# Gate arithmetic of a fused GateLoop + PReLU-MLP kernel: small operations from GpSimd to VectorE, the state decay from VectorE to ScalarE, first gates in halves, an early activation, a new order

## The chip, the core and the metric

The kernel runs on one core of a Trainium2 chip. The core has five engines with a queue each, and each queue runs strictly in its order: TensorE (PE; its weight loads are shown as PEld), VectorE (DVE), ScalarE (ACT), GpSimd (POOL) and SyncE (SP, which here issues the DMAs). The metric is the device time of one execution in microseconds, the median of several runs. One execution was also profiled, instruction by instruction; its trace begins at 0 and its last instruction ends at the span.

## What is computed

```python
# q, k, v, a_re, a_im: 4 batches x 8 heads x 768 tokens x 48
mag = np.sqrt(a_re * a_re + a_im * a_im)
scale = np.minimum(mag, 0.999) / (mag + 1e-06)
a_re_n, a_im_n = (a_re * scale, a_im * scale)
...
for t in range(S):
    new_re = ar * S_re - ai * S_im
    new_im = ar * S_im + ai * S_re
    kv = np.einsum('bhd,bhe->bhde', k[:, :, t], v[:, :, t])
    S_re, S_im = (new_re + kv, new_im)
    y[:, :, t] = np.einsum('bhd,bhde->bhe', q[:, :, t], S_re)
...
h = x @ w_in                                   # x: y as 3072 x 384; w_in: 384 x 2048
g = np.maximum(h, 0.0) + alpha * np.minimum(h, 0.0)
return (g @ w_out).astype(np.float32)          # w_out: 2048 x 384
```

A complex gate per head, token and feature makes a state decay and turn; each token adds its key-value product and reads the state with its query. The result goes through an MLP with a PReLU.

## The kernel before, in words

The program is a set of Python generators, each one a strand of work that stops at every `yield`. A long string `ORDER` (L30) names with one letter after another which strand goes on by one step (`Plan.run`, L99). So the order of each engine's queue is written out by hand, letter by letter; a wait between engines is a semaphore that the framework puts where a tile is read after it is written.

**Gates** (`gates`, L228) run nine times, called g0 to g8 here: 128, 256 and 384 tokens of batch 0, then two times 384 tokens of each other batch. One set has all 8 heads x 48 features on 128 partitions, in three groups, so 384, 768 or 1152 elements a partition. A set does, in this order: magnitudes and square roots (ScalarE L259 to L287, VectorE L265 to L307); a tree of decay products by halves (L324), sent to memory as `decs`; a running product of the turned unit numbers, first within 8 tokens (L344 multiplies, L346 adds, seven times), then over 8 such blocks (again seven times, 72 and 36 elements), then step by step along the blocks (12 and 6 elements, six times for 384 tokens), with ScalarE copies between (L372, L374); then the products for the offsets (L402, L405), a correction of length (L413, L415, L417), and at last the full phases (VectorE L432, L435), sent to memory as `phs`. What is at most `SMALL` = 80 elements a partition, and what is written with `tiny`, goes to GpSimd, except in g0, where it goes to VectorE:

```python
tiny, tiny_engine = (DVE, nc.vector) if g < 1 else (POOL, nc.gpsimd)
```

**Weights** (`to_f32`, L500) come as float64 words and are turned to float32 in 16 pieces, `w_in` and `w_out` in turn: ScalarE L513, L515, L517; GpSimd L521; VectorE L523, L525. The GpSimd step stands in the same queue as the small gate operations, and VectorE L523 waits for it.

**Units** (`unit`, L649) are the 24 blocks of 128 tokens, u0 to u23, six to a batch. Each loads phases (`PP`) and decays (`T`) from memory, turns queries and keys (VectorE L667, L669), then six times decays them by half-blocks (VectorE L722), with ScalarE copies (L745, L761) for TensorE's small products (L684) and masks (VectorE L707, ScalarE L698). The state is kept in `St`, twice a unit: multiplied by its decay on VectorE (L834, 96x384), then the key-value products from PSUM are added (VectorE L837). ScalarE copies the output (L863), and it goes through memory into the MLP's `xT`.

**The MLP** (`features`, L889) makes for each 128 or 256 tokens and each of 16 blocks of features three products on TensorE (L897), a Relu on ScalarE (L904) and the PReLU on VectorE (L906, 160 of them); the block's output product (L916) follows on TensorE. The last three groups of 256 tokens use sums of blocks in place of some products (L1016, L1028 to L1060, L1079, L1091). "The n-th PReLU" below is the n-th L906 in VectorE's queue.

Of the kernel before, what the change touches and what calls it, by code (L numbers as in the profile page):

```python
# [9 lines left out]
F32 = mybir.dt.float32  # L10
# [3 lines left out]
AF = mybir.ActivationFunctionType  # L14
# [16 lines left out]
    "AABMBAMAAJAJAAAAAAABMMJJAAAAABABAAKAAAAAABABAAAAKABAKABAMALNABLLABBBMLABBLABLBNKABOAKNNABAMAOANLBBAA"  # L31
    "AAOOAAAABMAANKBLAAABKAANAABAABAOBAAAANABABABABALNNAAKAOAAAAAOMAOKAAAOOAABABLNKBNBNCBNCBJBNNBJBJBLBBO"
    "BOBBBBNBCNBBCBPBCBBOCBPPLKMKKCBMCKBBPJBPCKKPPCJBBPOPOOBBBOMBLPPBBKCCBBJNOKBBJPKPKPBBPBNBBCBBBCCBBBCC"
    "PCPBCBOBNNCOMBBBPKBLOOPCMBBPCPBCNBPPPPPBCOOCONPDCNDCJCNCCCCCPPKOCLPCOPCCNNOCMCJDNJCJCDNDKCCPCDCCNCCK"
    "QDCMPDCCCPDCCPCNCPCPPOQPDCNLPLCCDCJNCDJPPPQLPLOQQLCPQCDNCCQMCCDLDCCJPOQCPPCQPCCJCDDLDLOLNOOnDLCCJQJD"
    "DLOQQLRQJoKOOOoJOoQLDKRCCCCCoCJCooooQQLCoQDCNoooQRoCCNCoLQRCCRoKRNNQJQQMQQoooooQDQQoQRDooQoQooCoQQDC"
    "DooQCoRRDQDNQOoRLLDNLRRoLRCoNLLooooRoLoNMooooQoLRRNNCLLRLKCRLRQCRRRoRRRLRLQLoQQQoDQoQQORQQDoQROoJoRD"
    "RoooORDJDJoDoRDoORoRDoOODRSoLJoDoESoJDJESLLRSSDnSOLDooDoSDoDJDDDDDoRLDSSDJDoSDKKooooSSRDoLENDLRRRDNK"
    "DoRRLRooooORDoRSoREooKSooELoSSJELoLooooooEooSJoLoEoTSLSDLoDSSDKSSDSLoooSKDTDoooooSSSJooooEoDTDJoETDD"
    "oooSoTSToDTDEEoEDooooSoDSTTDEDSESSoDLDooETLoooLSTLEDDDDoJDDDLSDoooTToooLSDJooTooLooLSSSTLSTooJEooLoo"  # L40
    "LSoooSToLSoDLoDoooSEooSToLTLooETTEDooJoTUTTJToTDooooTJoDoTnKEoooooTDoToooooDToTUDTTTDLLoooooULoLoooU"
    "oDLoJoLDooUoUDUooooJoUUJooooLoTEULoLooooUKoEUJoTULooEFoUoLoTLoEFUUELETTELUoooooToUVTUoooUUTTUTTUoTUo"
    "EEooooEoVoJoUJEUVooooUEJoUEJoEEooUoUooEUoEFUUEUoUFEoLELoFEoLoEJFEJEoELoooooEVLEoVJELUVLEoooooVFLVEUU"
    "EVLEUoLUooEoVVEoEUVoUEUUoUoooVEWVFEVoVoEEnEoJEVVEJEooooEoEFKVELoLooVEEVFKEoLoVVVVoLEoJVWEoooEKWEEVVK"
    "FLJooooVoWEEEFooooWWoWJEVoJoJooVWWoEVWoFoVWEVFFoEVEVoEFVVFWVLWLEWELoooLoVoLFoLLWWoLVVoEVWLoVVFoVVVoV"
    "oEFoLWoLWooLWWWWWoFLoELWLWWoJoEJoWXEoooooooEEJJEJoooWoWoooFEoooWoWEXWoWJWoXLoKoWXLWoLFoooWXLXWWGXWLo"
    "WFoGoXXWLXWWoLooooLXoFXJXWoXLoLFXXFFoooooFXFoLoGFLWFLooooXFXLoLXXXXoXXoFXGFoooXonXFoJFoJXoFXJoooFGJX"
    "FJGJXoFGooFYoGFooooooFXYFoFGFoooJYFXoXXLYFLXFFLXFXLFFLFFLFFoooYYooYYYooooXFXLFYoKXFoXFKGYFFoLXXooYYo"
    "XFYFXoLoYYoFFGFFoJGJYFLooooooLYFZoFFYLGLYFYJYYYLYoooooFYZJooGKoooZJYFoFYKoGFFFFoZLFZJoZYJZKYZZoooooG"
    "GoYoZYYGZYYFZLFZooLZLoGLooLoZZLGFoZGLFLGoooLYLoYGooooZZYLYYYoLooZZYZLoYZLZoYaYYoLZoFYZZFGoFZFoooaZoZ"  # L50
    "FoJoJZoFJZZoZFZoLLGoFFoLooFnoLaLLooooooaJFaoJaaLJGFaaGGooooooGLaLZGaLZoooooooaGoaZHZZZLaZJHoooLoaaoo"
    "ZaZoZZGZoooaoGaooGoaaaaaaoLoLaGGoooaoaKbooaoGHGooooJGaoHoGbbaKHaJaGJaoaGLHLLooooHoGLobLoGHLooobJoGoG"
    "LoaGGbGGGJbaobGHKaoGbGaJoLbboGKHGoLaaoLobGJKHHbGLoHLoooobboGLbaGoaaaobLbLooooHboJoGGcKobGbGGJbbbbGbJ"
    "bbJoooobGHGooboboGbGGobGHHGcGbobGHbGGboLcLonoHcoJoLcobcLGGGGGooGbJGocHJGoLoccoLGbLHLcoLbcLooooobHbLd"
    "cLcbobcbbbLoooobccoLoLGcHoJoHGJooccocccGccGoccJoHoGJcoJcGHGHooococoocoGHGJHcccooHdoodooGdoGooocodLdc"
    "GdoooLoHLoddLooooLdooodIooocLoHLocoIcdLoHdcLdcLcJoooddKoHcLcdoooccoooIcHLddHLoHIoLdoLIJeoJdddoooooJd"
    "HodKdIdodJoooJHdJodHoIoHdHIHddeodIdooJIoLLooHLeoHLHoHoooeHIHoIoooodKeHeodLHHdKHeHKHLdddHLooooHoeeHLo"
    "HeHLodLoooeofnHoHdLHedHHIeLHoeHddodeeHHooooHoHIeHoJoIHLJooooeIHIeLHoJoJeeeeeHoKeeIJJoooeoeoLoIooooII"
    "ofooHefJoHeHHoooffIHfeHfIHooffoIofoooeoefgoeHefLfIoLfoLoILeoILoooHffLoHgoLIoLoeHLooofLoIoIoeLfoeLfHe"
    "fffLHeffLfeIHeHeIeefooooHooefoIfLoooIoIoJoHJfofKoooJHoooIHHoJJooooHoofoIHffffIgLLoooLgoIgHgfoLgoLoLg"  # L60
    "gLoooIoJfoooogLoLoogfJfffgLgIfoLffgofffoLoIggLKogoooooLgIJgoIJggggIJIgIoJpggIooogogogogoIhIooggggIhh"
    "JJngIoLgoJIohLIogLIhoILLoogghIhLgIhgIogLhIgogohhoLiIgIoILhIoooooohJIiIhoLhLhIJooooLIhhoIILoIhIJoLooo"
    "IhLIhIJIhoIhooohoJhihhJhhoIIIJhooopIiohohiihiIoioiooooIioIohihIohIohjiLIiIoLiLoLohonioLoiLooohLohoLi"
    "oLoLhhhioIhiLhohihLioiIiIiohiohLoILoiiLiooopJooJoJioioooIooiIIiiiiijoLILoLjLLiooooooooojooJoILooLjiL"
    "jojJoIoooLjjoJojoLLiijiLjoijoLiojiLioLjiojioJojoooojjJojjjjJojjoJjpjoJjJooojojokojokjjojkjoLjLkojLkk"
    "JokoJoLkkLjoLkLjLkooojjojojojjjlkojkLooLokokkJkJoooooooooJooLkoLkoonkkkkkLokkJolookkolLLooookllklolo"
    "llooooooloklkokokkkokLLkoLkooLoLlolokLlkLoLlloLokJlkoJoLokoooJpLooLookooololoollkoLomkoLllLlooololpo"
    "loJoJplmooololoolollllmoooomlolomomoomoommoomoooomololomomolmlolmlolmoooonloooLmLoLoLmomooommmmLomoo"
    "LooLoooomoLoLoolooLoomLooooooqLooLooLoooooomomooooooooomoooooooooooooooooooomoooooooooooooooomomomoo"
    "moomooomomopomomoqlmqmqmmmqqmqqqooooooqoqooooqoqqoqooqqoqooqooqqqqooqqoooqoqooooqoqqoqooqqooooooooqo"  # L70
    "ooooooqoqooooooooooqooqoqoqqoqoooqonqqoqooqoqqooqoqoqqqqoqqooooooooooqoqqoooooooooqoooooooooqoqqoooo"
    "ooqoooooooqoqoqooqoqqqqoqqoooooooooooooooqqqoqoqoqqqoqoqooooooooqqoqqooooooooqqoqqoqooqooooooooqoqqq"
    "ooooooqoqqoqooqoqooqqoqooooqoooooooqoqqoooooooooooqooooqqoooqoqqoqooqoqooqqoqoqqqoqoooqqqqooqoooooqo"
    "qqoqooqoooqqooooooqoooooooooooqoqooooooooooooqqqqoqqoooooooooooooooqqqooqoqqoqqoqoqoqoooooooqooqqooo"
    "qqooooqoqqooooooooqooooqqooooooqqoqqooooooooqoooooooqoooqoqqqoqoooooooooqqqoqooooqoooqqoqqoqooqoqooq"
    "oqqqqqqqqqqqqqqqqqqqqqqqqqqq")
# [28 lines left out]
def kernel(  # L105
# [120 lines left out]
    nc.vector.memset(bias_half, -0.5)  # L226

    def gates(g, b, c0, c1):  # L228
# [8 lines left out]
        tiny, tiny_engine = (DVE, nc.vector) if g < 1 else (POOL, nc.gpsimd)  # L237
# [7 lines left out]
        flat = work.tile([P, 6 * NK * GT], F32, tag="gate", name="gate", bufs=2)[:, 0:6 * N]  # L245
# [3 lines left out]
        for z, src in ((x, a_re), (y, a_im)):  # L249
            z = z.rearrange("p (t s) -> p t s", t=NK)  # L250
            rows = src[b].rearrange("n i d s -> (n i d) s").rearrange("(t p) s -> p t s", p=P)
            t = yield DMA(N / 2, ("gates", g - 2))
            nc.sync.dma_start(z[:, :, 0:n - last], rows[:, :, c0 * P + 1:c1 * P + 1 - last])

        t = yield ACT(N, t)
        if last:
            ends_ = G[:, 0:6:5].rearrange("p r (t s) -> p r t s", t=NK)[:, :, :, n - 1]
            nc.scalar.activation(ends_, ident[:, 0:2 * NK].rearrange("p (r t) -> p r t", r=2), AF.Copy, scale=0.0)
        nc.scalar.activation(x, x, AF.Identity, scale=1.5, bias=bias_tiny)  # L259
        yield ACT(N)  # L260
        nc.scalar.activation(c, x, AF.Square, scale=GATE_SCALE)
        t = yield ACT(N, t)
        nc.scalar.activation(d, y, AF.Square, scale=1.5 * GATE_SCALE)
        t = yield DVE(N, t)
        TT(out=c, in0=c, in1=d, op=ALU.add)  # L265

        t = yield ACT(N, t)
        nc.scalar.activation(d, c, AF.Abs_reciprocal_sqrt)
        t = yield ACT(N, t)
        nc.scalar.activation(e, d, AF.Square)  # L270

        te = yield ACT(N, t)
        nc.scalar.activation(f, e, AF.Abs_reciprocal_sqrt)
        t = yield DVE(N, te)
        TT(out=e, in0=e, in1=c, op=ALU.mult)
        t = yield DVE(N, t)
        STT(out=d, in0=e, scalar=3.0, in1=d, op0=ALU.subtract, op1=ALU.mult)
        tf = yield ACT(N)
        nc.scalar.activation(f, f, AF.Square, scale=ONE / (1.5 * GATE_SCALE * MAG_EPS), bias=bias_one)
        tf = yield ACT(N)  # L280
        nc.scalar.activation(f, f, AF.Abs_reciprocal_sqrt)
        tf = yield ACT(N)
        nc.scalar.activation(f, f, AF.Identity, scale=ONE / 2.0, bias=bias_half)
        ts = yield DVE(N, t)
        TT(out=c, in0=c, in1=d, op=ALU.mult)
        ts = yield ACT(N, ts)
        nc.scalar.activation(c, c, AF.Copy, scale=1.0 / (1.5 * GATE_SCALE))  # L287

        L = 8
        nb = N // L  # L290
# [889 lines left out]
```

## Time and profile before

| | us |
|---|---|
| median of 3 runs (lowest, highest) | 836.75 (834.86, 837.43) |
| the profiled execution's own time | 839.4 |
| its span | 837.7 |
| busy PE / PEld / DVE / ACT / POOL | 689.3 / 544.4 / 695.3 / 441.3 / 321.6 |

A row of the profile's groups reads: line, engine, operation, tile written <- tiles read, shape written <- shape read, how many; then busy us and mean ns of one; then the engine's idle time ahead of them and what ended it. The part in 40 slices gives the busy share of each slice (20.9 us) in tenths. The chain of waits follows the work that ended last back from the end; a window of it is a list of start, duration, engine, tile and line. The view of waits gives for each engine and line what it waited for: us in total, times, the longest.

### The profile page before, as it was taken

What the parts mean: (1) busy time and instruction counts of PE and PEld (TensorE: products, weight loads), DVE (VectorE), ACT (ScalarE), POOL (GpSimd) and SP (SyncE); (2) the same over time, 40 slices, a digit from 0 to 9 for tenths busy, and PEclk for the clock granted to TensorE, in tenths of its full rate; (3) what the DMA queues carried; (4) which work ended last, traced back from release to release, by engine and by line L of the source; (5) the groups of instructions that cost most, each with busy time, mean ns of one, the idle gap of its engine ahead of it and who ended that gap; (6) DMA issues with size and microseconds to landing.
All of it is one profiled execution on the core that took longest, in us unless ns stands there. A gap on an engine that the chain in (4) does not pass through costs nothing.

```text
span 837.7 us, 27535 instructions
## 1 busy us (share of the span) xinstructions
PE 689.3 (82%) x11680; PEld 544.4 (65%) x11680; DVE 695.3 (83%) x1074; ACT 441.3 (53%) x946; POOL 321.6 (38%) x448
## 2 busy tenths in 40 slices
PE   0000225888999999999999999999999999999997
PEld 0000224666777777677766777777776777899997
DVE  5977978999898999899998999998897676546574
ACT  8767777557556746673666477344433334212121
POOL 5378397448203800860193037216100000324332
PEclk9999999899999999999999999999999999999999
DMA  6793876695686679548875875687466442100000
GB/s 186 222 266 120 279 210 154 216 224 143 170 247 143 178 191 259 137 124 236 216 203 123 249 174 152 174 214 187 98 189 146 125 119 58 34 27 20 1 20 20
DMA packets 186595, 130.97 MB, mean 156 GB/s; under 512 B 74728, under 2 KB 176872, under 8 KB 186088
## 3 DMA queue, kind: packets, MB, share of 16 engines
q1 hardware_dynamic: 186472, 129.20, 57.4%
q8 instruction: 92, 1.51, 0.8%
q14 instruction: 31, 0.25, 0.1%
HBM read 100.82 MB, written 35.71 MB: 163 GB/s over the span
## 4 chain that ended last, share of the span: by engine, by line
PE 55%; DVE 22%; POOL 12%; ACT 5%; issue 4%; DMA 2%; DVEq 0%; ACTq 0%; POOLq 0%; SPq 0%
PE ps_o L916 16%; PE ps_h L897 15%; PE ps_m L1091 6%; DVE KQ L722 4%; POOL gate L344 4%; PE ps_lv L684 4%; PE ps_y L1016 3%; PE ps_h L1016 3%; DVE gate L344 3%; POOL run L346 3%; POOL gate L346 3%; PE ps_y L825 2%; DVE gate L346 2%; PE ps_y L849 2%; PE ps_kv L805 2%
## 5 line engine op out<-in xcount | busy, mean ns | idle before, releaser
L916 PE MATMUL ps_o<-w_out_sb,g_sb 128*128 128x384 f32 x576 | 226.7, 510 | 7.4 <-DVE g_sb L906 7.3
L897 PE MATMUL ps_h<-xT,w_in_sb 128*128 128x256 f32 (+1 forms) x960 | 228.0, 369 | 0.0
L897 PEld LDWEIGHTS ps_h<-xT,w_in_sb 128*128 128x128 f32 x960 | 172.7, 195 | 49.4 <-issue 3.1
L722 DVE TENSOR_TENSOR KQ<-KQ,T 96x1024 f32<-96x1024 f32 x120 | 148.7, 1239 | 23.4 <-PE ps_lv L684 17.1
L916 PEld LDWEIGHTS ps_o<-w_out_sb,g_sb 128*128 128x128 f32 x576 | 103.9, 194 | 48.3 <-DVE g_sb L906 8.6
L904 ACT ACTIVATE g_sb<-ps_h 128x256 f32<-128x256 f32 (+1 forms) x160 | 57.5, 361 | 104.7 <-PE ps_h L897 104.1
L684 PE MATMUL ps_lv<-WQ 96*32 96x32 f32 x2304 | 35.0, 204 | 78.0 <-DVE WQ L667 53.4
L1079 POOL TENSOR_TENSOR sums<-g_sb 128x128 f32<-128x128 f32 x48 | 21.8, 475 | 192.0 <-DMA ysc<-T 117.5
L684 PEld LDWEIGHTS ps_lv<-WQ 96*32 96x32 f32 x2304 | 26.7, 116 | 99.2 <-DVE WQ L667 53.4
L906 DVE SCALAR_TENSOR_TENSOR g_sb<-g_sb,al,ps_h 128x256 f32<-128x256 f32 (+1 forms) x160 | 71.1, 445 | 22.2 <-ACT g_sb L904 20.5
L344 POOL TENSOR_TENSOR gate<-gate 128x72 f32<-128x72 f32 (+1 forms) x56 | 35.0, 626 | 140.7 <-ACT gate L374 102.6
L745 ACT COPY WQ<-KQ 96x1024 f32<-96x1024 f32 x48 | 50.0, 1041 | 27.0 <-DVE KQ L722 26.8
L324 POOL TENSOR_TENSOR gate<-gate 128x72 f32<-128x72 f32 (+5 forms) x24 | 13.1, 547 | 109.1 <-DVE gate L324 102.6
L761 ACT COPY W<-KQ 96x512 f32<-96x512 f32 x48 | 30.8, 641 | 42.7 <-DVE KQ L722 36.6
L684 PE MATMUL ps_lv<-KQ,W 96*32 96x32 f32 x1536 | 24.8, 206 | 33.4 <-ACT W L761 33.2
L521 POOL TENSOR_SCALAR top<-top 128x768 f32<-128x768 f32 x16 | 41.8, 2617 | 23.7 <-ACT top L513 23.7
L344 DVE TENSOR_TENSOR gate<-gate 128x576 f32<-128x576 f32 (+3 forms) x70 | 46.1, 659 | 1.1
L825 PE MATMUL ps_y<-A,VL 64*48 64x64 f32 x2304 | 41.8, 221 | 5.4 <-issue 5.4
L344 POOL TENSOR_TENSOR gate<-run,runs 128x12 f32<-128x12 f32 x46 | 39.3, 854 | 15.0 <-ACT runs L374 11.7
L432 DVE TENSOR_TENSOR gate<-gate 128x1152 f32<-128x1152 f32 (+2 forms) x36 | 44.7, 1263 | 0.1
L825 PEld LDWEIGHTS ps_y<-A,VL 64*48 64x48 f32 x2304 | 38.8, 123 | 8.9 <-issue 8.8
L684 PEld LDWEIGHTS ps_lv<-KQ,W 96*32 96x32 f32 x1536 | 20.2, 116 | 35.2 <-ACT W L761 34.7
(157 smaller groups left out, 1435.6 us busy)
## 6 DMA issues: line engine op xcount, KB each, us to landing
T<-decs SPq DMA_DIRECT2D x48, 384.0 KB
PP<-phs SPq DMA_DIRECT2D x24, 387.0 KB
KQ<-in_q_dram SPq DMA_DIRECT2D x48, 192.0 KB
decs<-gate SPq DMA_DIRECT2D x7, 1152.0 KB
phs<-gate SPq DMA_DIRECT2D x14, 576.0 KB
KQ<-in_k_dram SPq DMA_DIRECT2D x40, 192.0 KB
vsc<-in_v_dram SPq DMA_DIRECT2D x48, 144.0 KB
VL<-vsc SPq DMA_DIRECT2D x48, 144.0 KB
```

The source lines that it names most:

```text
L344: on(4 * k).tensor_tensor(out=m, in0=w[:, 1::-1].unsqueeze(2).to_broadcast([P, 2, 2, k]), in1=pairs_of(u), op=ALU.mult)
L346: on(2 * k).tensor_tensor(out=dst, in0=m[:, 0], in1=m[:, 1], op=ALU.add)
L684: nc.tensor.matmul(t[64 * i + j:64 * i + j + HC // 2, p], lhsT=keys(n, g), rhs=queries(n, g), start=True, stop=True)
L722: nc.vector.tensor_tensor(out=x, in0=x if x0 is None else x0, in1=m, op=ALU.mult)
L745: nc.scalar.copy(z.rearrange("p i n t -> p i (n t)").rearrange("p i (m h) -> p m i h", h=h), bass.AP(tensor=KQ.tensor, offset=KQ.offset + ...
L825: nc.tensor.matmul(o, lhsT=Vp[h][64 * i:64 * i + 64, s, e_ * D:(e_ + 1) * D], rhs=a, start=False, stop=False)
L897: nc.tensor.matmul(p, lhsT=w_in_sb[:, f // 2, kk, f % 2 * P:(f % 2 + 1) * P], rhs=x_of[m][:, kk], start=(kk == 0), stop=(kk == NK - 1))
L904: nc.scalar.activation(gt, p, AF.Relu, scale=-1.0)
L906: nc.vector.scalar_tensor_tensor(out=gt, in0=gt, scalar=al_1[:, f:f + 1], in1=p, op0=ALU.mult, op1=ALU.add)
L916: nc.tensor.matmul(sums[0], lhsT=gt[:, c * P:(c + 1) * P], rhs=w_out_sb[:, f], start=(f == 0), stop=(f == NF - 1))
L1016: nc.tensor.matmul(o, lhsT=lhs, rhs=rhs, start=(at in (0, 5)), stop=(at in (4, 8)))
L1091: nc.tensor.matmul(banks[k][:, half], lhsT=lhs, rhs=rhs, start=(j == 0 and half == 0), stop=(j == NF // 2 - 1 and at in (2, 3, 5, 6)))
```

## The change

1. `tiny` is VectorE for every set. With it all operations of L324 to L417 that ran on GpSimd go to VectorE; GpSimd keeps the small memset L311, the weights' L521 and the late sums L1079.
2. g0 (384 elements) is worked in two halves of 192 for the magnitude and the root; its `x` no longer waits for `a_im`; the copies of the unit numbers come in six halves, ahead of what the decays need.
3. Sets of 128 and 256 tokens make the unit numbers ahead of the decays; g1's three rows then lie in a part of the gate tile of their own.
4. An activation of one column (`Abs_reciprocal_sqrt`) is the first instruction of ScalarE.
5. From unit 4 on the state times its decay is made by eight ScalarE activations of 96x48, one per head, with the decay as scale, in place of L834.
6. `ORDER` is another string, so that every queue has a new order.

```diff
+    nc.scalar.activation(consts.tile([P, 1], F32, tag="first", name="first"), bias_two, AF.Abs_reciprocal_sqrt)
...
-        tiny, tiny_engine = (DVE, nc.vector) if g < 1 else (POOL, nc.gpsimd)
+        tiny, tiny_engine = DVE, nc.vector
...
+            for h in range(2):
+                yield from enter(h)
+            for h in range(2):
+                yield from root(h)
...
-        U5 = G[:, 0:3].rearrange("p r (m n i) -> p r m n i", m=L // 2, i=2)
+        U = G[:, 0:3] if C > 2 else flat_[:, 6 * N:9 * N].rearrange("p (r n) -> p r n", r=3)
+        U5 = U.rearrange("p r (m n i) -> p r m n i", m=L // 2, i=2)
...
+            def enter(h):
+                x, c, f, d, e, y = parts[h]
+                yield ACT(N // 2, tx)
+                nc.scalar.activation(x, x, AF.Identity, scale=1.5, bias=bias_tiny)
...
-            k_ = yield DVE(H * D, known, takes=(R["St"],))
-            St = work.tile([D2, H, D], F32, tag="St", name="St", bufs=3)
-            nc.vector.tensor_tensor(out=St, in0=before, in1=T[0:D2, :, TL - 4 + s:TL - 3 + s].to_broadcast([D2, H, D]),
-                                    op=ALU.mult)
+            if u < 4:
...
+            else:
+                k_ = yield ACT(5 * H * D, known, takes=(R["St"],))
+                St = work.tile([D2, H, D], F32, tag="St", name="St", bufs=3)
+                for n in range(H):
+                    nc.scalar.activation(St[:, n], before[:, n], AF.Copy, scale=T[0:D2, n, TL - 4 + s:TL - 3 + s])
```

## The prediction

> **What bounds the kernel now.** First the part in 40 slices, to see which engine is full when.
>
> ```profile
> PE   0000225888999999999999999999999999999997
> ...
> DVE  5977978999898999899998999998897676546574
> ...
> POOL 5378397448203800860193037216100000324332
> ```
>
> TensorE is nearly idle for six slices (to about 126 us), then full to the end. VectorE is full between about 140 and 600 us too, and has holes before. So two questions count: when TensorE's full stretch begins, and whether VectorE can feed it. From the first PReLU (138.2 us) to the end are 699.5 us; TensorE's rows behind that point, each at its group's mean and scaled to the 689.3 us busy, are 679. From the 37th PReLU (243.4 us) on 593 us of work stand against 594.3: **from there nothing is lost any more**. Both orders have, within 3 us, the same TensorE work behind each PReLU. So the time is that of the 37th PReLU plus 594.3, if VectorE keeps up after it.
>
> Next, the chain of waits in the window 88 to 140 us, to see why TensorE begins so late (start, us, engine, tile, line).
>
> ```profile
> 118.71 0.24 POOL gate L344
> ...
> 119.02 5.47 POOL run L346
> ...
> 124.56 2.09 POOL gate L344
> ...
> 129.53 2.10 POOL top L521
> ...
> 131.66 0.03 DVE top L523
> ...
> 135.37 1.42 DVE KQ L722
> ...
> 138.15 0.34 DVE g_sb L906
> ```
>
> From 104 to 131.6 us all of it is GpSimd: g2's small operations, one by one, and behind them in the same queue the weights' L521, for which VectorE's L523 waits, with unit 1 and the PReLUs behind it. The waits of VectorE between 53 and 140 us give the price:
>
> ```profile
> DVE top L523 <- POOL top L521: 10.2, 3, 3.9
> DVE gate L307 <- ACT gate L287: 4.6, 1, 4.6
> ```
>
> Then the groups by shape, for what an operation costs on each engine:
>
> ```profile
> L346 POOL TENSOR_TENSOR run<-gate 128x6 f32<-128x6 f32 x46 | 39.5, 858 | 3.6
> ...
> L344 POOL TENSOR_TENSOR gate<-gate 128x72 f32<-128x72 f32 x49 | 28.6, 584 | 137.2 <-ACT gate L374 102.6 <-ACT A L698 31.3
> ```
> ```profile
> L834 DVE TENSOR_TENSOR St<-St,T 96x384 f32<-96x384 f32 x44 | 25.4, 578 | 0.2
> ...
> L344 DVE TENSOR_TENSOR gate<-gate 128x24 f32<-128x24 f32 x7 | 1.3, 181 | 0.2
> ...
> L346 DVE TENSOR_TENSOR run<-gate 128x6 f32<-128x6 f32 x2 | 0.3, 164 | 0.0
> ```
> ```profile
> L698 ACT ACTIVATE A<-ps_lv,columns 128x64 f32<-128x64 f32 x96 | 23.3, 315 | 9.5 <-PE ps_lv L684 9.3
> ```
>
> The same 6-element addition takes 858 ns on GpSimd in the mean (0.20 us at its shortest, 5.46 at its longest) and 164 on VectorE.
>
> **How a queue is summed.** VectorE's instructions overlap a little. In the timeline:
>
> ```profile
> 28.82 0.18 DVE L344 TENSOR_TENSOR gate<-gate 128x24 f32<-128x24 f32 x1
> 28.92 0.95 DVE L525 CUSTOM_DVE_ANT_0 w_in_sb<-top,w_in_sb 128x1536 uint16<-128x1536 uint16 x1
> 29.79 0.16 DVE L346 TENSOR_TENSOR gate<-gate 128x12 f32<-128x12 f32 x1
> ```
>
> The next instruction begins about 0.085 us before the end of one that it does not need; where it needs it, about 0.035 after. So I add each instruction's mean by its row, less 0.085 or plus 0.035. Shapes with no VectorE row lie between neighbours (12 elements 0.167, 24 0.181, 48 0.208, 96 0.255, 144 0.298, 288 0.46): 72 are put at 0.23, 36 at 0.195, 252 at 0.42. The queue ahead of three points, with the orders as the two strings give them:
>
> - unit 1's L667: before 84.1 us of work, begun at 104.1; after 80.7.
> - first PReLU: before 107.8, at 138.2; after 110.6.
> - 37th PReLU: before 206.8, at 243.4, so 36.6 of waiting; after 224.4.
> - 129th PReLU: before 518.3, at 581.5; after 547.0.
>
> **The change part by part.**
>
> *Small operations.* 293 leave GpSimd, where gate work falls by about 225 us busy; on VectorE they are about 66 us of durations (gate rows 237 to 303), some 8.5 us for a set of 384 tokens: 7 x (0.23 + 0.195) + 6 x (0.17 + 0.165) + 0.6 for L324 + 2.9 for the rest. That is in the sums above: +17.6 at the 37th PReLU, +28.7 at the 129th. What goes: L523's 10.2 us of waiting, since GpSimd then has little but L521; and the longer VectorE instructions beside GpSimd's (L307 of 768 elements took 1.61 us where its neighbours L285 and L304 took 0.95). With medians instead of means the sum ahead of the 37th is 4.4 us less, of which I take 4. Late next: ScalarE, whose copies feed the small products.
>
> *Early activation, halves.* ScalarE's two table loads took 1.28 us each, at 3.53 and 6.43, both ahead of g0's root; now one is left, beside the DMA's landing. [...] Halves cost: 0.355 + 0.355 against 0.555, six times on VectorE, +0.9; as much twice over on ScalarE. And the decay tree (1.9 us) now stands ahead of the first L344. Followed instruction by instruction: first L344 at about 16.8 (before 15.5), second seven products from 24.8 (26.0), last L435 at about 40.0 (40.2). So unit 0 begins at about 51.5 against 52.1: worth nothing alone, since the phases' way through memory hides it.
>
> *g1.* Its operations on GpSimd reached from 49.1 to 77.3 us; behind unit 0's start VectorE has 29 us up to g1's last L435, with ScalarE copies about 83.7 against 87.0; unit 1 about 96 against 104. L307's 4.6 us of waiting goes as well: ScalarE's L287 then stands at about 72, its reader at 86.
>
> *State on ScalarE.* 36 of 44 L834 leave VectorE: 20.8 us, in the sums. ScalarE gets 288 activations of 48 elements. No such row exists; below 128x6 (188 ns, L424), above 128x64 with a scale from memory (243 a piece, 23.3/96): 54 to 70 us, I take 0.23, so 66. They lie beside PE; 46 us net of overlaps, ScalarE 441 of 838 before. Behind each block of eight (1.8 us) the Relus and copies wait. Hidden while ScalarE has 30% idle; if not, it falls on TensorE (below).
>
> *SP.* The same DMAs; the loads of `PP` for unit 0 move ahead of g2's two loads, up to 1.2 us of issue, which I leave in the 51.5.
>
> **The sum.** Waiting ahead of the 37th PReLU: 36.6 - 10.2 (L523) - 4.6 (L307) - 4.0 (longer instructions) - 3.0 (L906 waiting for ScalarE between 140 and 245 us, as TensorE is then ahead) + 1 (new small waits) = 15.8. So 224.4 + 15.8 = 240.2, 3.2 us earlier. The step from there to the 129th needs 322.6 of VectorE in 338.1, so TensorE goes on bounding it. 837.7 - 3.2 = 834.5 of span; the profiled execution's 839.4 stands 2.65 above the median, which gives **833.5 us**.
>
> **Rivals.**
>
> 1. *VectorE's queue takes it back* (slower). VectorE has 114 us of work between the first and the 37th PReLU in place of 99, and TensorE 86: there VectorE bounds. It decides if more than 19 us of waiting is left ahead of the 37th. For it: each of the five turns to ScalarE and back in a set now stops VectorE's whole queue where before it stopped GpSimd's (L344 there waited 102.6 us for L374). Against it: of VectorE's 16.6 us idle between 53 and 134 us, the two waits shown are 14.8. With 25 us left: 249.4, +6, and 1 us of pile-up between two full engines: 844. If all waiting of before came again, 224.4 + 36.6 = 261, 854.
> 2. *Nothing*: the earlier start is eaten exactly by the longer queue, 240.9 to 245.9 at the 37th: 836.8.
> 3. *ScalarE* (slower): TensorE already waited 18.0 us for L761's copies between 130 and 600. If one in nine of 36 blocks delays one by 1.8 and a copy of 0.6, that is 9.6 us: 843. [...]
> 4. *Faster still*: VectorE stops only for its first input and for unit 0's phases, 11 us as before unit 0: 235.4, 828.7.
> 5. *The change doesn't do what it says*: excluded by the order, in which GpSimd keeps 121 rows of 425.
>
> **Chances.** Forecast with rival 4, waits gone: 0.46. Nothing: 0.20. VectorE's queue: 0.25. ScalarE: 0.09. About 0.3% (2.5 us) is what a measurement here can tell from no change. So faster 0.46, same 0.20, slower 0.34. Range 824 to 846: below, rival 4 with all of the 4.4 us that the medians take off; above, rival 1 with 2 us more of waiting. The 854 is left out.
>
> **What would show it.** GpSimd near 97 us busy, VectorE near 730, ScalarE near 490. L523's 10.2 us gone; unit 0 at 51 to 53 us, unit 1 near 96, the first PReLU (29.9 us of work behind that) near 128, the 37th near 240. If the first is early and the 37th is not before 243, rival 1 holds. If TensorE's waits for L761 and L745 grow after 243 us, rival 3. I'm wrong at the root if the first PReLU is not earlier.

## The result and the profile after

The changed kernel takes 843.59 us (median of six runs, 839.86 to 847.07) against 836.63 before (834.86 to 837.43, six runs): a ratio of 1.0081, 95% interval 1.0055 to 1.0108. So it is slower, where 833.5 was forecast. The profiled execution took 843.07 us, its span is 841.4, 3.7 more than that of before. Busy are PE 695.9, DVE 716.2, ACT 505.6, POOL 95.8 us. (A ratio leaves out the executions that took over 1.5% longer than the fastest of the same kernel: one of six in a4, two of eleven in a5, three of six in a6, one of eight in a9; so it can stand below that of the medians.)

In the lines of the changed kernel 344 is 416, 346 is 418, 521 is 593, 523 is 595, 667 is 739, 722 is 794, 745 is 817, 761 is 833, 825 is 897, 834 is 907 (ScalarE: 913), 837 is 915, 897 is 975, 904 is 982, 906 is 984 and 916 is 994.

The 40 slices:

```profile
PE   0003139758999989898999999989999999999997
...
DVE  5999999998998989897999999979998775546574
...
POOL 6141332100000000000000000000000000324333
```

TensorE's first work comes one slice earlier, and the seventh slice is a 9 where it was a 5; then it has holes: a 7 and a 5 right behind, and eights in the stretch that was nines. VectorE is full from the second slice. Windows show it in numbers, first before, then after; the columns are the stretch, its length, then busy us of PE, PEld, DVE, ACT, POOL, the granted clock, the DMA share and GB/s:

```profile
60.00:100.00 40.00, 4.40 (x136) 3.30 (x136) 32.32 (x39) 29.46 (x43) 27.42 (x28) 1.00 0.57 179
100.00:140.00 40.00, 13.91 (x339) 12.05 (x340) 31.80 (x34) 28.85 (x42) 32.36 (x38) 1.00 0.75 211
```
```profile
60.00:100.00 40.00, 11.01 (x364) 9.40 (x364) 39.19 (x60) 30.20 (x46) 9.29 (x5) 0.85 0.72 209
100.00:140.00 40.00, 22.87 (x507) 18.01 (x508) 38.62 (x59) 33.54 (x51) 12.74 (x5) 0.59 0.73 202
140.00:200.00 60.00, 40.16 (x822) 30.89 (x824) 59.07 (x105) 35.39 (x77) 5.53 (x2) 0.86 0.74 195
```

The chain of GpSimd's small operations is gone from 88 to 140 us; what is left of GpSimd there is one piece of the weights (the chain of waits, after):

```profile
112.51 3.36 POOL top L593
115.90 0.56 DVE top L595
...
120.61 1.35 DVE gate L380
121.96 1.30 DVE gate L416
123.25 0.27 DVE g_sb L984
```

The last line is the first PReLU, at 123.2 us instead of 138.2. VectorE's waits between 53 and 140 us are down to 1.4 us:

```profile
DVE gate L416 <- ACT gate L446: 0.7, 1, 0.7
DVE gate L269 <- ACT gate L267: 0.4, 2, 0.2
DVE g_sb L984 <- ACT g_sb L982: 0.3, 1, 0.3
```

What the moved operations cost, by shape:

```profile
L913 ACT ACTIVATE St<-St,T 96x48 f32<-96x48 f32 x288 | 68.7, 324 | 6.8 <-DVE St L915 6.8
...
L416 DVE TENSOR_TENSOR gate<-gate 128x72 f32<-128x72 f32 x49 | 11.0, 225 | 0.9 <-ACT gate L446 0.7
...
L418 DVE TENSOR_TENSOR run<-gate 128x6 f32<-128x6 f32 x48 | 7.9, 164 | 0.7
```

So far this is much as forecast. What is new and lost is in one row. Before, then after, from the groups:

```profile
L825 PE MATMUL ps_y<-A,VL 64*48 64x64 f32 x2304 | 41.8, 221 | 5.4 <-issue 5.4
```
```profile
L897 PE MATMUL ps_y<-A,VL 64*48 64x64 f32 x2304 | 43.3, 222 | 15.0 <-issue 15.0
```

The same 2304 small products have 15.0 us of idle TensorE ahead of them, and what ended it is "issue": no engine, no DMA of the kernel. The timeline of TensorE shows one of the seven stalls. It lies inside a run of equal products, whose data were all there:

```profile
196.78 0.95 PE L897 MATMUL ps_y<-A,VL 64*48 64x64 f32 x55
199.75 0.81 PE L897 MATMUL ps_y<-A,VL 64*48 64x64 f32 x41 [2.01 <-issue]
```

Counted through the trace, TensorE's instruction behind each of these stalls has the number 193 + 256n (3521 at 199.75 us); a block is here the 256 instructions up to such a number. The profile lists a DMA queue of its own for instructions:

```profile
q8 instruction: 92, 1.51, 0.8%
```

92 packets of 1.51 MB are 16 KB each; TensorE has some 23,630 instructions, which is 92.3 times 256. Each of the seven stalls ends 1.3 to 1.6 us after such a packet has landed (here 198.3, the products go on at 199.75). So I read it that TensorE has run out of instructions; the experiments test that. A stall costs more than its idle time: behind four of the five stalls of 2 us and more the granted clock is half for 3.4 us (from 200.8, 340.8, 388.5 and 552.4; before: behind the one of 1.9 us that ends at 637.9, from 638.9, but not behind the one of 2.1 us that ends at 107.6), and the two L994 that begin at 200.49 take 1.37 us where two at 190.78 took 0.91.

**Where the time went.** "Stalls" are here the idle times of over 0.3 us ahead of the numbers 193 + 256n, less 0.06 each; the tail is the time from the 37th PReLU to the span's end. All from the profiled executions, in us:

| kernel | 1st PReLU | 37th PReLU | span | tail | stalls in the tail | tail without |
|---|---|---|---|---|---|---|
| before | 138.2 | 243.4 | 837.7 | 594.3 | 5.3 | 589.0 |
| changed | 123.2 | 243.1 | 841.4 | 598.3 | 13.9 | 584.4 |
| changed, a0 | 124.7 | 244.5 | 838.6 | 594.1 | 10.0 | 584.1 |
| a5, shift 16 | 124.5 | 241.4 | 837.3 | 595.8 | 8.5 | 587.3 |
| a3, shift 24 | 125.6 | 243.1 | 844.9 | 601.8 | 12.8 | 589.0 |
| a8, shift 228 | 124.6 | 245.9 | 850.7 | 604.8 | 17.6 | 587.2 |
| before, a4, shift 184 | 136.7 | 244.4 | 848.9 | 604.5 | 16.9 | 587.6 |
| before, b4, shift 12 | 138.3 | 243.8 | 832.3 | 588.5 | 4.6 | 583.9 |
| a7, 9.1 us more at u0 | 134.4 | 251.8 | 850.4 | 598.6 | 12.6 | 586.0 |
| before, b2, the same | 146.8 | 253.2 | 844.2 | 591.0 | 6.3 | 584.7 |
| a2, state on VectorE | 125.1 | 243.2 | 846.4 | 603.2 | 12.6 | 590.6 |
| b1, small operations alone | 136.2 | 245.9 | 845.9 | 600.0 | 5.0 | 595.0 |

Other ways of measuring the same gaps move a sum of stalls by about 1 us. Without the stalls the tails of both orders are 584 to 589 us, a2 and b1 aside. The 15 us that the first PReLU gains are used up at the 37th, and behind it 8.6 us more of stalls stand against 4.6 us less of everything else.

### The profile page after: what moved, and what is told of

It is laid out like the page before. It is cut to its first block, busy times and chain, and to the rows that moved or that the text cites. A ratio compares the mean times of both kernels' runs of the same rounds, so it can differ in the third digit from the quotient of the medians.

```text
span 841.4 us, 27800 instructions
## 1 busy us (share of the span) xinstructions
PE 695.9 (83%) x11680; PEld 545.6 (65%) x11680; DVE 716.2 (85%) x1343; ACT 505.6 (60%) x1243; POOL 95.8 (11%) x149
## 3 DMA queue, kind: packets, MB, share of 16 engines
q8 instruction: 92, 1.51, 0.8%
## 4 chain that ended last, share of the span: by engine, by line
PE 67%; DVE 15%; ACT 6%; DMA 6%; issue 3%; SPq 2%; POOL 0%; DVEq 0%; ACTq 0%
PE ps_o L994 20%; PE ps_h L975 18%; PE ps_m L1169 6%; PE ps_lv L756 5%; PE ps_y L897 4%; PE ps_h L1094 3%; PE ps_y L1094 3%; DVE KQ L794 3%; PE ps_kv L877 3%; PE ps_y L927 2%; DMA T<-decs 2%; DVE gate L504 2%; DVE gate L416 2%; PE ps_kt L865 2%; DVE gate L418 1%
## 5 line engine op out<-in xcount | busy, mean ns | idle before, releaser
L975 PE MATMUL ps_h<-xT,w_in_sb 128*128 128x256 f32 (+1 forms) x960 | 230.1, 372 | 10.2 <-DMA xT<-ysc 7.4
L994 PE MATMUL ps_o<-w_out_sb,g_sb 128*128 128x384 f32 x576 | 229.7, 515 | 6.1 <-DVE g_sb L984 5.6
L975 PEld LDWEIGHTS ps_h<-xT,w_in_sb 128*128 128x128 f32 x960 | 173.3, 197 | 60.5 <-DMA xT<-ysc 8.2
L794 DVE TENSOR_TENSOR KQ<-KQ,T 96x1024 f32<-96x1024 f32 x120 | 146.1, 1217 | 23.0 <-PE ps_lv L756 16.0
L994 PEld LDWEIGHTS ps_o<-w_out_sb,g_sb 128*128 128x128 f32 x576 | 104.3, 195 | 48.0 <-DVE g_sb L984 7.3
L982 ACT ACTIVATE g_sb<-ps_h 128x256 f32<-128x256 f32 (+1 forms) x160 | 57.8, 361 | 95.1 <-PE ps_h L975 94.1
L984 DVE SCALAR_TENSOR_TENSOR g_sb<-g_sb,al,ps_h 128x256 f32<-128x256 f32 (+1 forms) x160 | 71.4, 447 | 20.1 <-ACT g_sb L982 19.5
L913 ACT ACTIVATE St<-St,T 96x48 f32<-96x48 f32 x288 | 68.7, 324 | 6.8 <-DVE St L915 6.8
L416 DVE TENSOR_TENSOR gate<-gate 128x576 f32<-128x576 f32 (+5 forms) x126 | 58.7, 466 | 1.7 <-ACT gate L446 0.7
L593 POOL TENSOR_SCALAR top<-top 128x768 f32<-128x768 f32 x16 | 41.7, 2610 | 105.9 <-ACT top L585 105.9
L897 PEld LDWEIGHTS ps_y<-A,VL 64*48 64x48 f32 x2304 | 39.9, 123 | 17.9 <-issue 17.6
L504 DVE TENSOR_TENSOR gate<-gate 128x1152 f32<-128x1152 f32 (+2 forms) x36 | 43.0, 1231 | 0.1
L833 ACT COPY W<-KQ 96x512 f32<-96x512 f32 x48 | 30.8, 641 | 19.8 <-DVE KQ L794 17.2
L418 DVE TENSOR_TENSOR gate<-gate 128x288 f32<-128x288 f32 (+5 forms) x126 | 41.2, 327 | 1.3
L770 ACT ACTIVATE A<-ps_lv,columns 128x64 f32<-128x64 f32 x144 | 37.6, 333 | 7.1 <-PE ps_lv L756 7.0
```

The costliest lines, as they stand in the source:

```text
L416: on(4 * k).tensor_tensor(out=m, in0=w[:, 1::-1].unsqueeze(2).to_broadcast([P, 2, 2, k]), in1=pairs_of(u), op=ALU.mult)
L504: TT(out=m[:, a], in0=U5[:, 1 + a], in1=turned(off3, o)[:, a].unsqueeze(1).unsqueeze(3).to_broadcast([P, L // 2, nb, 2]), op=ALU.mult)
L794: nc.vector.tensor_tensor(out=x, in0=x if x0 is None else x0, in1=m, op=ALU.mult)
L897: nc.tensor.matmul(o, lhsT=Vp[h][64 * i:64 * i + 64, s, e_ * D:(e_ + 1) * D], rhs=a, start=False, stop=False)
L913: nc.scalar.activation(St[:, n], before[:, n], AF.Copy, scale=T[0:D2, n, TL - 4 + s:TL - 3 + s])
L975: nc.tensor.matmul(p, lhsT=w_in_sb[:, f // 2, kk, f % 2 * P:(f % 2 + 1) * P], rhs=x_of[m][:, kk], start=(kk == 0), stop=(kk == NK - 1))
```

## Experiments

Three theories. **Q**: VectorE's queue uses up the early start. **F**: TensorE's instruction blocks come late; how often depends on where the blocks' ends fall among its bursts. **S**: the state's decay on ScalarE holds TensorE up.

### Shifting TensorE's instructions (a3, a8, a0 with a5; before: a4, b4)

```diff
         plan.add(late_outputs())
+        p0 = ps.tile([P, MT], F32, tag="h", name="ps_h", bufs=2)
+        for _ in range(6):      # a5: 4, a8: 57; the kernel before: a4 46, b4 3
+            nc.tensor.matmul(p0[0:32, 0:32], lhsT=ident[:, 0:32], rhs=ident[:, 0:32], start=True, stop=True)
         plan.run(ORDER)
```

> The changed kernel with six unused products of 32x32 (four TensorE instructions each) put in front, so that every later TensorE instruction has a number that is 24 higher; nothing else is changed, and the output is the same. Theory F (TensorE's instructions arrive in blocks of 256, and where a block is worked off in under about 3.8 us while the DMA engines are busy, TensorE stands until the next has landed: 15.0 us in seven stalls, all at number 193 of 256): the stalls fall on other places; from the time that each block of 256 took and the DMA load beside it I reckon some 5 us less of them, so 836 to 841, and stalls at numbers that lie 24 later in the old count. Theory Q (VectorE's full queue is all that took the gain back): the same time as the changed kernel, 843 to 844, within 1.5 us, and the stalls move without the end moving.

> The kernel before with 46 unused products of 32x32 in front, 184 TensorE instructions, in the idle time ahead of the first unit; nothing else is changed, and the output is the same. Theory F: the old stalls of 6.4 us go and others come, reckoned at 15 to 18 us more, so 846 to 854. Theory Q: 836 to 838, as before, since neither VectorE's nor ScalarE's queue is touched. A result of under 840 speaks against F as a mechanism that is worth microseconds.

> The changed kernel with 57 unused products in front, 228 TensorE instructions; output the same. Theory F: by the time of each block of 256 and the DMA load at its end this is the worst place of all, some 14 to 20 us of stalls more than in the changed kernel: 855 to 865. Theory Q: 843 to 844. Beside that, if the unused products bring the stretch of half clock forward, as 46 of them did in the kernel before (8 to 104 us there), the first PReLUs run at full clock; by theory Q that is worth nothing at the 37th PReLU, which stays at 243 plus the stalls ahead of it.

Ratios to before: a3 1.0040 (1.0010 to 1.0069), a4 1.0138 (1.0103 to 1.0172), a8 1.0240 (1.0204 to 1.0276); medians 839.24, 849.36 and 857.60 us. The kernel before becomes 13 us slower by nothing but 46 unused products in its idle first microseconds, the changed one 14 us slower by 57 and, by the medians, 4 us faster by 6. Theory Q expected no difference in any of the three. a4's trace accounts for its time: of 11.2 us more span 10.2 lie in the tail, with 11.6 us more of stalls. a8's does so only in part: its profiled execution, the fastest of four, has 9.3 us more span, but 3.7 us more of stalls in the tail and 0.8 ahead of it, not the 14 to 20 that were reckoned. a4's row and one of its longest stalls, in a burst that the kernel before runs through in one piece (its line comes last):

```profile
L825 PE MATMUL ps_y<-A,VL 64*48 64x64 f32 x2304 | 44.5, 225 | 15.3 <-issue 15.3
```
```profile
382.48 1.44 PE L825 MATMUL ps_y<-A,VL 64*48 64x64 f32 x88
...
387.10 0.40 PE L825 MATMUL ps_y<-A,VL 64*48 64x64 f32 x8 [3.19 <-issue]
```
```profile
380.41 1.55 PE L825 MATMUL ps_y<-A,VL 64*48 64x64 f32 x96
```

The changed kernel had not run beside a3, and a3's times scatter (835.32 to 846.57). Its profiled execution is the slowest of them, and its stalls are only 1.1 us fewer in the tail (12.8 against 13.9), not the 5 that were reckoned; so the gain of a3 is not shown by its trace. The changed kernel was run once more, with another shift beside it on the same chip:

> The changed kernel once more, unaltered, on the same chip as the next one: 843 to 844 by its six earlier runs (839.9 to 847.1). It serves as the base for the next kernel.

> The changed kernel with four unused products in front, 16 TensorE instructions; output the same. Theory F: by the blocks' times in six traces of this TensorE order this is the best of all places, 10 us of stalls against 16 as it stands: 4 to 7 us less than the changed kernel on the same chip, 836 to 840. Theory Q, or chance in the run of 24: the same as the changed kernel within 2 us.

a0 1.0099 (1.0072 to 1.0127), 845.12 us; a5 1.0040 (1.0016 to 1.0064), 841.11 us. The medians are 4.0 us apart, at the lower end of the 4 to 7 that were reckoned, and so are the ratios' middles (0.6%). But the ranges overlap (840.32 to 848.06 and 834.45 to 848.82), and the means of all executions, 844.50 and 841.48, lie 3.0 apart: a gain from four unused products is likely, not certain. Among the shifts it is a4, whose time and trace agree, that carries the argument. The same row in a0 and in a5:

```profile
L897 PE MATMUL ps_y<-A,VL 64*48 64x64 f32 x2304 | 43.9, 224 | 10.0 <-issue 10.0
```
```profile
L897 PE MATMUL ps_y<-A,VL 64*48 64x64 f32 x2304 | 42.0, 221 | 7.1 <-issue 7.1
```

> The kernel before with three unused products in front, 12 TensorE instructions; output the same. Theory F: reckoned from the blocks' times, about 2.5 us less of stalls than as it stands (5.7 against 8.2): 832 to 836. Theory Q: 836.5. A result above 838 would show that the reckoning of places is no better than chance where the differences are small.

b4: 836.54 us, 1.0012 (0.9990 to 1.0033). No gain: the reckoning tells good places from bad ones, not two good ones apart. It can't confirm or refute F.

### Is it the DMA load? (d1)

In 17 traces there are 1505 block ends behind 115 us. Sorted by how long TensorE took for the block before, and by the DMA engines' mean load in the last 3 us of it:

| block worked off in | load under 0.4 | 0.4 to 0.65 | over 0.65 |
|---|---|---|---|
| under 4 us | 48, mean 0.46 us, 18 stalls over 0.6 | 25, 0.43, 6 | 85, 1.75, 62 |
| 4 to 5.5 us | 103, 0.04, none | 52, 0.02, none | 128, 0.26, 18 |
| over 5.5 us | 327, 0.05, none | 268, 0.07, 4 | 469, 0.04, 2 |

That is a correlation. d1 makes the load:

```diff
+                if (u, i) == (5, 0):
+                    for r in range(2):
+                        copy = dram.tile([96, 4096], U32, tag="copy", name="copy", bufs=2)
+                        nc.sync.dma_start(copy, w_in.bitcast(U32)[96 * r:96 * (r + 1)])
                 nc.sync.dma_start(KQ[rows, 0], qv[b, :, :, cols])
```

> The kernel before with two copies of 1.6 MB each of the weights from memory to unused memory, issued at 197.6 us; output the same. The number 3521 (193 of 256) of TensorE is reached at about 204 us, the block before it worked off in 2.7 us, and the DMA engines are idle from 201 to 203.5: no stall there in three traces of this order (0.08 to 0.5 us). Theory F with the DMA load as a cause: a stall of 1 to 3 us at that number, behind an instruction transfer that lands late. If only the rate of TensorE counts and not the DMA load: 0.1 to 0.5 us as before. The time is of less use, as the copies also delay the loads behind them: 836 to 842.

TensorE at this place before, and in d1:

```profile
203.34 1.67 PE L825 MATMUL ps_y<-A,VL 64*48 64x64 f32 x96
```
```profile
202.80 0.99 PE L829 MATMUL ps_y<-A,VL 64*48 64x64 f32 x54
205.80 0.83 PE L829 MATMUL ps_y<-A,VL 64*48 64x64 f32 x42 [2.01 <-issue]
```

A new stall of 2.2 us stands exactly at number 3521, and another of 2.1 us at the next block's end, 3777 (211 us); the first one's packet landed at 204.5. So the load is a cause; that TensorE's rate is another rests on the table alone. The time is 841.56 us, 1.0069 (1.0048 to 1.0091).

The queue's packets show how. In the changed kernel the packet for the next block starts 1.0 us (median of 92) after TensorE has passed the block end before, takes 1.15 us in the mean, and TensorE goes on 1.3 to 1.6 us after it has landed: an estimate of 3.5 us from these three, and by it a block that is worked off faster would wait; in the table 86 of the 158 blocks of under 4 us did. In the seven stalls, behind blocks of 2.1 to 3.8 us, the packet started 1.0 to 4.5 us after the block end before. At number 3521 it started 0.5 us after in the kernel before and 2.7 us after in d1.

Behind the first PReLU the changed kernel's stalls come to some 17 us (13.9 in the tail, 2.2 at 199.75 and 1.1 at 230.03).

### VectorE's queue at the start (a7, b2)

```diff
+        for _ in range(9 if u == 0 else 1):
             nc.vector.tensor_tensor(out=WQ, in0=some(1, -1), in1=phases(1, 0), op=ALU.mult)
```

> The changed kernel with unit 0's first product on VectorE (L739, 1.22 us) written nine times instead of once: 8 x 1.135 = 9.1 us of extra VectorE work at about 49 us; output the same. Theory Q: VectorE has no room between 50 and 243 us (busy 39.2 of 40 us from 60 to 100, 38.6 of 40 from 100 to 140, 59.1 of 60 from 140 to 200), so the 37th PReLU comes 7 to 9 us later, at 250 to 252, and the time is 850 to 853. If TensorE, the DMAs or ScalarE bounded that stretch, part of the 9 us would be swallowed: 37th PReLU at 243 to 247, time 843 to 847.

> The kernel before with the same 9.1 us of extra VectorE work at unit 0 (L667 nine times), at about 53 us; output the same. Theory Q: there VectorE has room (busy 32.3 of 40 us from 60 to 100, 31.8 of 40 from 100 to 140) behind the chain of GpSimd, so most of it is swallowed ahead of the first PReLU: 37th PReLU 0 to 4 us later, time 836 to 840. If VectorE's queue were as tight in the kernel before, 844 to 846.

a7: 855.26 us, 1.0230 (1.0204 to 1.0257), 37th PReLU at 251.8, 8.7 later, as Q expects; the time is above its 850 to 853, the profiled execution's 852.06 within. b2: 846.77 us, 1.0107 (1.0080 to 1.0134), 37th at 253.2, 9.8 later: Q's expectation for the kernel before was wrong. Its VectorE was busy only 32.3 of 40 us there, but g1's phases come 8.7 us later all the same, and with them the GpSimd chain behind: the holes are VectorE's waits in a chain that it stands in itself, so nothing is swallowed. The start is serial in both kernels: what unit 0 loses is lost at the 37th PReLU, and about as much at the end.

### The parts alone (b1, a1, a2, a6, b3, a9)

```diff
-        tiny, tiny_engine = (DVE, nc.vector) if g < 1 else (POOL, nc.gpsimd)
+        tiny, tiny_engine = DVE, nc.vector          # b1, on the kernel before; a1 is the reverse, on the changed one
...
-            if u < 4:
+            if u < NU:                              # a2; in a6 u < 0; b3 puts u < 4 and its branches into the kernel before
```

> The kernel before, with one line changed: all small gate operations on VectorE; old order, whole first gates, state decay on VectorE; output the same. Theory Q: ahead of the 37th PReLU 206.8 + about 20 us of VectorE's work and 16 to 19 of waiting, 243 to 246, so the start is no earlier; ahead of the 129th 518 + 46 = 564 of 581 us, so VectorE bounds up to there: 838 to 848. The theory of the forecast (VectorE keeps up and the early gain stays): 833 to 835. Theory F adds or takes up to 6 us by chance to either, as the times at which blocks are worked off shift; the trace shows how much.

b1: 846.83 us, 1.0127 (1.0103 to 1.0151). The 37th PReLU is at 245.9 and the tail without stalls 595.0, 6 us over before's: TensorE's waits for VectorE there are 5.8 us (before: 1.4), so VectorE bounds in part, as Q says. The small operations alone, in the old order, are a loss of 10 us.

> The changed kernel with one line back: the small gate operations of all sets but the first on GpSimd again, in the new order; output the same. Theory Q (the start is one serial chain through VectorE's queue and what it waits for): VectorE's 17.6 us of small operations ahead of the 37th PReLU go, but GpSimd's chain of g2 (27 us in the kernel before) comes back ahead of it in an order that leaves less room for it, so the 37th PReLU is at 245 to 260 and the time 846 to 862. If moving the small operations was a loss in itself, the time is under 841.

a1: 854.88 us, 1.0215 (1.0173 to 1.0256), 37th PReLU at 248.7. VectorE's waits for L593 are back (4.6 us between 53 and 140 us). In the new order the move to VectorE is worth 10 to 11 us; in the old one it costs 10.

> The changed kernel with the state's decay on VectorE for all units (36 operations of 578 ns back, 288 activations gone); output the same. Theory Q: VectorE, full between 60 and 240 us, gets about 1 us more ahead of the first PReLU (units 4 and on come later), some 5 us ahead of the 79th PReLU and 21 in all, so 844 to 852, and the 37th PReLU 1 to 5 us later. Theory S (ScalarE's activations delay the copies that TensorE waits for): 836 to 840, and TensorE's waits for L833 and L817 shrink. Theory F alone: 843 to 844, as the number of TensorE instructions does not change.

a2: 848.47 us, 1.0148 (1.0111 to 1.0185), some 5 us slower than the changed kernel; its tail without stalls is 590.6 instead of 584.4. So the state on ScalarE is a gain here, and S falls. The 37th PReLU stays at 243.2; Q expected it 1 to 5 us later.

> The changed kernel with the state's decay on ScalarE for all 24 units instead of from the fifth on (8 operations of 578 ns leave VectorE ahead of the 37th PReLU, 64 activations of some 0.24 us come to ScalarE); output the same. Theory Q (VectorE's queue is what sets the 37th PReLU): that PReLU 2 to 4 us earlier, at 239 to 241, and the time 840 to 842, with theory F's noise of 2 on top. If ScalarE's early chain is the bound there instead, the 37th PReLU stays or comes later: 843 to 846.

a6: 1.0116 (1.0071 to 1.0161), not faster: Q's expectation of 2 to 4 us was wrong. Its profiled execution took 854.87 us, so only a wait is read from it: up to 250 us L915 waits 4.7 us in four places for L913, about what VectorE was relieved of.

> The kernel before with the fifth point of the change alone: the state's decay on ScalarE from unit 4 on; old order; output the same. In the changed kernel the opposite step cost 5 us. Here VectorE is not the bound behind the 37th PReLU, and ahead of it only units 4 and 5 gain, 4 x 0.49 = 2 us less of VectorE's work against up to 1.3 us for each wait of the addition for the block of eight on ScalarE (as with all units on ScalarE). So nothing much: 834 to 839. A theory in which VectorE also bounds behind the 37th PReLU in the old order gives 828 to 832; one in which the blocks on ScalarE hold TensorE up gives 840 to 845.

b3: 855.63 us, 1.0226 (1.0191 to 1.0260): 19 us slower than before, where all theories stayed within 9. VectorE's waits between 160 and 700 us, of b3 and then of the changed kernel:

```profile
DVE St L843 <- ACT St L841: 33.9, 21, 5.1
DVE g_sb L912 <- ACT g_sb L910: 24.1, 26, 3.3
```
```profile
DVE St L915 <- ACT St L913: 1.3, 2, 0.8
```

The same 288 activations cost 68.6 us on ScalarE in both. In the old order the addition stands right behind in VectorE's queue, and the queue stops 21 times until ScalarE has come to its block of eight; in the new order only twice. I read it that this makes the fifth part pay; the orders differ in more than that, and the new order was never run without the other parts.

> The changed kernel with the first gates worked whole instead of in halves and without the early activation; all else as changed; output the same. By the prediction these parts bring unit 0 forward by nothing or 1.3 us. Theory Q (the start is serial, as 9.1 us more at unit 0 came out as 8 to 10 us at the end in both kernels): what unit 0 loses, the 37th PReLU and the end lose, so if unit 0 goes from 47.9 to 49 to 52 us, the time is 844 to 848. If the start has slack, unit 0 is later and the 37th PReLU is not.

```diff
-    nc.scalar.activation(consts.tile([P, 1], F32, tag="first", name="first"), bias_two, AF.Abs_reciprocal_sqrt)
...
-                nc.scalar.activation(x, x, AF.Identity, scale=1.5, bias=bias_tiny)
+                if h:
+                    nc.scalar.activation(x, x, AF.Identity, scale=1.5, bias=bias_tiny)   # x whole; so for all steps of g0
```

a9: 847.11 us, 1.0110 (1.0076 to 1.0143); 1st PReLU at 126.2 and 37th at 245.9, 3.0 and 2.8 later than in the changed kernel; unit 0 begins at 50.7 us, 2.8 later. The halves and the early activation are worth about 3 us in the trace; the times (interval over 5 us wide) agree with that but do not prove it.

## Why the prediction was wrong, point by point

- **The mechanism at the start was right, and larger than forecast.** L523's 10.2 us and L307's 4.6 are gone; unit 0 began at 47.9 us (forecast 51.5), unit 1 at 91.2 (96), the first PReLU at 123.2 (128). Unit 0 gained 4.2 us where I had forecast 0.6, "worth nothing alone"; a9 shows that 2.8 of them come from the halves and the early activation, and that they reach the 37th PReLU.
- **The prices of the parts were right, two totals were not.** Small operations: 68 us of durations on VectorE (66). State: 68.7 us (66), 21.0 us off VectorE (20.8). GpSimd 95.8 busy (97). VectorE 716.2 (730; I had added durations and forgot that they overlap); ScalarE 505.6 (490; the "46 us net of overlaps" came as 64).
- **The waiting ahead of the 37th PReLU was 18.7 us instead of 15.8** (243.1 - 224.4). The full queue was forecast well: between the first and the 37th PReLU VectorE was busy for 114.1 of 119.9 us, TensorE for 97.9. The term "- 3.0 (L906 waiting for ScalarE ... as TensorE is then ahead)" failed. VectorE's L984 still waits 3.1 us for L982 up to 250 us, and 2.6 of it is this one:

```profile
203.48 0.35 DVE L984 SCALAR_TENSOR_TENSOR g_sb<-g_sb,al,ps_h 128x128 f32<-128x128 f32 x1 [2.60 <-ACT g_sb L982]
```

  It lies behind the TensorE stall of 197.74 to 199.75 that is shown above: the next L975 end there only at 203.1, at half clock. So F took this term, too.
- **The step that failed is "So the time is that of the 37th PReLU plus 594.3, if VectorE keeps up after it".** VectorE kept up: TensorE waits 1.1 us for it behind the 37th PReLU (before 1.4). But the reading under the 594.3, that "593 us of work stand against 594.3" and so "nothing is lost any more", was wrong. Windows from the 37th PReLU to the end, before and after, give TensorE 577.4 busy us of 594.3, so 16.9 idle, and 579.3 of 598.3:

```profile
243.40:837.70 594.30, 577.36 (x9289) 455.20 (x9288) 485.12 (x753) 277.31 (x660) 182.46 (x286) 0.99 0.53 139
```
```profile
243.10:841.40 598.30, 579.33 (x9240) 455.65 (x9240) 490.10 (x904) 337.46 (x929) 43.40 (x100) 0.99 0.53 137
```

  A count of instructions times their groups' means hid this idle time. TensorE's waits there:

```profile
PE ps_lv L684 <- ACT W L761: 6.0, 3, 2.7
PE ps_y L825 <- issue: 3.3, 2, 1.9
PE ps_lv L684 <- issue: 1.2, 2, 1.0
```
```profile
PE ps_y L897 <- issue: 12.1, 5, 3.4
PE ps_kv L877 <- ACT T L868: 0.9, 1, 0.9
...
PE ps_lv L756 <- ACT W L833: 0.2, 1, 0.2
```

  So the 594.3 took for granted that the stalls of the old order (5.3 us) would stay as they were. They became 13.9. The row with 5.4 us of "issue" was in the profile of before, and I left it unread. How many stalls an order meets is in part luck: unused products alone move the old order's from 4.6 to 16.9 and the new one's from 8.5 to 17.6.
- **The sum of the profiled spans closes.** Forecast 834.5, measured 841.4: +2.9 at the 37th PReLU, +4.0 behind it (+8.6 stalls, -4.6 of everything else: L761's waits fell by 5.8, while TensorE's busy time rose by 2.0). The medians lie 7.0 apart where the profiled executions lie 3.7 apart; only profiled executions show stalls, and they vary (a0 has 3.9 us less in the tail than the same kernel's first profile, and is 2.8 us shorter). So the stalls are likely what makes one kernel's runs scatter by 7 us, but that isn't shown, and the 3.3 us by which the medians lie further apart than the profiled executions stay open.
- **The rivals.** *Nothing* (rival 2) describes the start best: the longer queue eats the earlier start, with the 37th PReLU between 240.9 and 245.9. But it gave 836.8, and the stalls came on top. VectorE's queue (rival 1) forecast the time, 844, and the landmark, a 37th PReLU not before 243. But it needed over 19 us of waiting, and its price came from 25 us and a 37th PReLU at 249.4; there were 18.7, and the loss came later, so it was right by its number and wrong by its cause. ScalarE (rival 3) is refuted: TensorE's waits for L833 fell, and a2 is slower. That a new order could move instruction blocks into worse places was none of my rivals.

## What to carry to other kernels

Read "issue" rows of the bounding engine: if they lie inside a burst of equal, short instructions, count the instructions in the trace and see whether the stalls share a number modulo the block size (here all seven stand at 193 modulo 256). The new order of this tightly packed kernel drew new places for its block ends (5.3 us of stalls in the tail became 13.9); unused instructions in front, in several different numbers, show how much of a difference is only that, though gains of 3 to 4 us were hardly told from the scatter here. Before an engine is called full, read its busy time over the stretch: a sum of group means gave 593 us where the trace has 577. And whether work that is moved to another engine pays can hang, as I read it, on where its reader stands in its own queue: the same 288 activations were worth 5 us in one order and cost 19 in the other.

## What the runs showed of the hardware that was not expected

- Beside TensorE's 23,631 instructions the trace of the changed kernel has 92 packets of 16 KB on a DMA queue for instructions, which is 256 instructions (one block) to a packet. TensorE stood in seven places, all at 193 + 256n, for 0.9 to 3.4 us, where it had worked off the block before in 2.1 to 3.8 us. In the table such stalls are more frequent the more the DMA engines are loaded (62 of 85 blocks of under 4 us at a load of over 0.65, 18 of 48 under 0.4), and in d1 two copies put one of 2.2 us where there was none. Behind the 37th PReLU the stalls are 4.6 to 17.6 us of some 840 in the kernels of the table.
- TensorE's granted clock was half for 44 us (88 to 132) in the changed kernel and for 96 us (8 to 104; by the slices below mostly on to 127) in a4, whose unused products ran at the very start; in the profiled execution of before it was half for at most 6.8 us at a time (from 161.0), but for 34 us (109 to 143) in b4, the same kernel with three unused products. The slices, after and a4:

```profile
PEclk9999558879999999999999999999999999999999
```
```profile
PEclk6555556889999999999989999999999999999999
```

  a4's first PReLU came at 136.7 all the same (before: 138.2), so it cost nothing on the path there. What sets these long stretches off stays open. The short ones of 3.4 us begin within 1.1 us of the end of an idle time of TensorE: the four of the changed kernel at stalls, as said above, the three of before at idle times of 3.4, 2.7 and 1.9 us (178.1, 440.9 and 638.9).
